# First product of the last token group as seven block products on operand sums, interleaved with the second product of the group ahead

## The chip, the cores and the metric

One NeuronCore of a Trainium2 chip runs the whole program. The metric is the device time of one execution in microseconds, as the median of several runs. A profile is one further execution, with a start and an end for each instruction.

## What is computed

Two stages. The first is an attention with exponential feature maps over 8 batches, 8 heads, 576 positions and 64 columns. The second works on its result, 4608 tokens of 512 numbers:

```python
def _moe_ref(x, g_ln, w_ch1, w_ch2):
    mu = np.mean(x, axis=-1, keepdims=True)
    var = np.mean((x - mu) ** 2, axis=-1, keepdims=True)
    xn = (x - mu) / np.sqrt(var + 1e-06) * g_ln
    ch = np.maximum(xn @ w_ch1, 0.0) @ w_ch2
    return x + ch
```

`w_ch1` is 512 x 2048 and `w_ch2` 2048 x 512. The change concerns the product `xn @ w_ch1` for one ninth of the tokens.

## The kernel before

The tokens form nine groups of 512 (`g` = 0 to 8; `MIX` = 7 holds the last 64 positions of every sequence, `LAST` = 8). Attention for later heads and the two products of earlier groups run interleaved; from about 301 us on only group 7's and group 8's products are left.

**First product** (`first(g, jj)`, L1423 to L1451). The 2048 hidden columns are 16 blocks `jj` of 128. For each block TensorE multiplies four 128x128 pieces of `w1` (one per 128 input numbers) with four 128x512 pieces of the transposed tokens `xT`, summing in one PSUM bank of pool B (`hT_ps`, L1429). ScalarE or VectorE applies the relu on the way to SBUF (L1437, L1439), into `ring`, which holds 24 blocks; the division by the deviation comes later, as the factor `rstd`.

**Second product.** For groups 6, 7 and 8 (`FAST`) it is already done with seven products for eight blocks, after Winograd's form of Strassen's scheme (`fast`, L1537 to L1643). The hidden index is split into even and odd blocks, the output columns into halves of 256, and the token tiles into pairs `p` = 0, 1. `weight_sums` makes four sums of `w2` blocks once, `token_sums` (L1514, instructions on L1531) makes for each pair four sums of `ring` blocks, in two halves of four instructions of 128x512 each. A step `i` = 0 to 6 is eight matmuls of 256 columns (L1594); steps 0 and 1 are split in two halves of four. After each step VectorE multiplies a PSUM range by `rstd` and adds it to the output tile (L1603). For group 7 both PSUM banks of a pair form one tile of pool A, and a later step of the pair waits for VectorE's reading of that tile. Group 7 and 8 each have 28 half or whole pieces, 112 matmuls.

**Order of the work.** The program records operations with the data that they read and write, and a planner (`Order.run`, L365) with assumed durations puts them into one fixed sequence for each engine before the kernel is built. Operations have a rank; `RELU` is the most urgent one. On the chip each engine follows its sequence strictly and waits on semaphores where data or a bank isn't ready. Pool B has three PSUM banks, `n_bank` is one bank, pool A two pairs of banks.

`moe(g)` lists the work. For group 8 it alternates `first(8, jj)` with pieces of `fast(7, ...)`; group 8's token sums come in two halves, after block 8 and after block 15. Then `fast(8, ...)` ends the program, with the output stores on the queues of SyncE and ScalarE. Each output tile of 128 tokens takes one of four slots (`out_pool`), free again when its store is through.

Of the kernel before, what the change touches and what calls it, by code (L numbers as in the profile page):

```python
# [10 lines left out]
FP32 = mybir.dt.float32  # L11
BF16 = mybir.dt.bfloat16
AF = mybir.ActivationFunctionType
ALU = mybir.AluOpType
# [11 lines left out]
RELU = -983.1  # L26
# [300 lines left out]
class Order:  # L327
# [163 lines left out]
def kernel(  # L491
# [27 lines left out]
    HG = 2  # L519
# [17 lines left out]
    EARLY = 8  # L537
    SHARED = 0
    XB = 3
    QB = 4  # L540
    NB16 = 3
    NW = 4
# [15 lines left out]
    ps_B = ctx.enter_context(tc.tile_pool(name="ps_B", bufs=3, space=bass.MemoryType.PSUM))  # L558
# [9 lines left out]
    qx_bufs = [consts.tile([P, TG, 2, D], FP32, name=f"qx{i}") for i in range(2)]  # L568
# [22 lines left out]
    vx_bufs = [consts.tile([P, TG, 2, D1], FP32, name=f"vx{i}") for i in range(2)]  # L591
# [19 lines left out]
    ea_bufs = []  # L611
# [6 lines left out]
    w1_sb = consts.tile([P, KC, DH], BF16, name="w1")  # L618
# [777 lines left out]
    ring = consts.tile([P, HB, RN], BF16, name="hT")  # L1396
# [17 lines left out]
    hT, hkey, ch = {}, {}, {}  # L1414

    def turn_of(g):

        return rk("moe", (H // 2 if g == 0 else H) - 1) if g < NR else counts["V"]

    def due(g, share):  # L1420
        return DUE + BLOCK * (g + share)

    def first(g, jj):  # L1423
        st = {}

        def products():
            st["ps"] = ps_B.tile([P, RN], FP32, tag="B", name="hT_ps")
            for kc in range(KC):
                nc.tensor.matmul(  # L1429
                    st["ps"], w1_sb[:, kc, jj * P : (jj + 1) * P],  # L1430
                    xT_bufs[g % XB][:, kc::KC, :], start=(kc == 0), stop=(kc == KC - 1),
                )

        def relu(engine):
            hT[g, jj] = h_sb = ring[:, slot, :]
            if engine == "DVE":
                nc.vector.tensor_relu(h_sb, st["ps"])  # L1437
            else:
                nc.scalar.activation(h_sb, st["ps"], AF.Relu)  # L1439
# [57 lines left out]
    def weight_sums():  # L1497

        B11, B12 = w2_sb[:, 0::2, 0:FH], w2_sb[:, 0::2, FH:DM]
        B21, B22 = w2_sb[:, 1::2, 0:FH], w2_sb[:, 1::2, FH:DM]  # L1500
        T1, T2, T3, T4 = T_of
        todo = ((T1, B12, B11, ()), (T2, B22, T1, (0,)), (T3, B22, B12, ()), (T4, B21, T2, (1,)))
        for i in range(2):
            add("SP", 0.0, RELU, None, w=[*S_home[i], ("S home", i)])
            add("SP", 0.0, RELU, None, w=[*T_home[i], ("T home", i)])
        for i, (out_, a, b, reads) in enumerate(todo):
            for c in range(0, CP, SH):
                def emit(engine, out_=out_, a=a, b=b, cs=slice(c, c + SH)):
                    eng = nc.vector if engine == "DVE" else nc.gpsimd
                    eng.tensor_tensor(out=out_[:, cs], in0=a[:, cs], in1=b[:, cs], op=ALU.subtract)  # L1510

                add(("DVE", "POOL"), (Port(0.6), 2.0), (), emit,
                    r=[("w2", m) for m in range(NW)] + [("T2", j, c) for j in reads]
                    + [("T home", i // 2)], w=[("T2", i, c)])  # L1514

    def token_sums(g, c):

        for p in range(NM // 2):
            def blocks(i, odd, p=p):
                s = (g * JC + 2 * c) % HB + odd  # L1520
                return ring[:, s : s + 2 * SH - 1 : 2, (2 * p + i) * P : (2 * p + i + 1) * P]

            def sums(i, p=p, blocks=blocks):
                S1, S2, S3, S4 = [t[:, c : c + SH] for t in S_of[p]]
                out_, a, b, op = (
                    (S1, blocks(1, 0), blocks(1, 1), ALU.add),
                    (S2, S1, blocks(0, 0), ALU.subtract),
                    (S3, blocks(0, 0), blocks(1, 0), ALU.subtract),
                    (S4, blocks(0, 1), S2, ALU.subtract),
                )[i]  # L1530
                nc.vector.tensor_tensor(out=out_, in0=a, in1=b, op=op)  # L1531

            for i, reads in ((0, ()), (1, (0,)), (3, (1,)), (2, ())):
                add("DVE", Port(0.32), (), lambda i=i, f=sums: f(i),
                    r=[hkey[g, jj] for jj in range(2 * c, 2 * c + 2 * SH)]
                    + [("S", p, j, c) for j in reads] + [("S home", p)], w=[("S", p, i, c)])

    def fast(g, p, i, cs):
# [104 lines left out]
        elif final:  # L1643
            dma("SP", counts["V"], 262144, lambda: store(g, t, ch["o", g, t]), r=both)

    def moe(g):


        done = 0
        if g == FAST[0]:  # L1650
            weight_sums()
        for jj in range(JC):
            if g <= LAST:
                first(g, jj)
            if g - 1 in FAST:
                pairs_, h1, h2 = range(NM // 2), range(SH), range(SH, CP)
                steps = [(p, i, cs) for cs in (h1, h2) for p in pairs_ for i in range(2)]
                steps += [(p, i, range(CP)) for i in range(2, 7) for p in pairs_]
                until = min(len(steps), -(-(jj + 1) * len(steps) // 8))
                for step in steps[done:until]:  # L1660
                    fast(g - 1, *step)
                done = until
            if g in FAST and jj in (SH * 2, JC - 1):
                token_sums(g, 0 if jj < JC - 1 else SH)
            if g - 1 in FAST:
                continue
            until = min(NM * JC, -(-(jj + 1) * NM * JC // AHEAD_H))
            while g > 0 and done < until:
                i, j0 = divmod(done, JC)
                n = min(until - done, JC - j0)  # L1670
                second(g - 1, i, j0, n)
                done += n
# [183 lines left out]
```

## Time and profile before

| what | value |
|---|---|
| median of 3 runs | 360.21 us (359.09 to 360.39) |
| profiled execution | 359.27 us |
| its span, first to last instruction | 357.5 us |
| around the span | 1.77 us |
| mean granted clock of TensorE | 0.998 |

The profile names engines PE (TensorE), PEld (TensorE's weight loads), DVE (VectorE), ACT (ScalarE), POOL (GpSimd) and SP (SyncE). A group row gives line, engine, instruction, output and inputs, then count, busy time and mean ns of one, and the idle time of the engine just before with what ended it. Durations of instructions that follow one another can overlap: a matmul's row lasts longer than the distance to the next one, and so do VectorE's. What counts for a sum is the distance.

### The profile page before, as it was taken

Reading aid. Unit: us, or ns where it says so; the run is one execution under the profiler, and the core shown is the slowest. Engines: PE = TensorE matmul, PEld = TensorE weight load, DVE = VectorE, ACT = ScalarE, POOL = GpSimd, SP = SyncE. Lnnn points to the kernel's source line nnn. Section 1 sums busy time; section 2 is a strip of 40 time slices with the busy share of each in tenths; the row PEclk is TensorE's granted clock in tenths of the full one; section 3 lists DMA queues with packets and bytes.
Section 4 is the critical chain, followed back from the end, with each engine's and each line's share of the span. In section 5 each row is a group of like instructions: output and inputs, shape, how many; then the busy total and the mean of one; then the engine's idle time right before and its main releaser. Section 6 shows DMA issues by size and latency. Waiting matters only on the chain.

```text
span 357.5 us, 9189 instructions
## 1 busy us (share of the span) xinstructions
PE 348.8 (98%) x3555; PEld 215.5 (60%) x3580; DVE 282.0 (79%) x605; ACT 255.0 (71%) x550; POOL 196.7 (55%) x249
## 2 busy tenths in 40 slices
PE   8999999999999999999999999999999999999995
PEld 8888855555554555455545555555555577457684
DVE  5699989799998888878789999887777897335463
ACT  3998977598988897969696985796788834652320
POOL 5389756596865876648579798465646410000000
PEclk9999999999999999999999999999999999999999
DMA  8999999999996877489629442831041006200503
GB/s 207 308 202 278 205 261 260 242 244 236 296 268 188 199 194 211 114 189 224 193 71 211 64 109 71 171 103 35 9 119 61 3 9 170 67 0 0 119 2 118
DMA packets 93676, 53.89 MB, mean 151 GB/s; under 512 B 61104, under 2 KB 88048, under 8 KB 93632
## 3 DMA queue, kind: packets, MB, share of 16 engines
q1 hardware_dynamic: 89392, 47.72, 55.5%
q0 software_dynamic: 3328, 4.49, 7.2%
q10 hardware_dynamic: 912, 1.08, 1.0%
q8 instruction: 28, 0.46, 0.5%
q14 instruction: 16, 0.13, 0.1%
HBM read 36.77 MB, written 9.44 MB: 129 GB/s over the span
## 4 chain that ended last, share of the span: by engine, by line
PE 79%; DVE 9%; DMA 6%; issue 2%; ACT 2%; SPq 1%; POOL 0%; DVEq 0%
PE hT_ps L1429 30%; PE ch_ps L1461 23%; PE ch L1594 9%; PE pm L988 4%; PE n_bank L1139 3%; PE num L1197 3%; DMA qk<-in_q_dram 2%; PE pt L997 2%; DMA qx<-in_k_dram 2%; DMA out_dram<-o 2%; DVE numc L1219 2%; DVE m L1045 2%; PE n_bank L1133 1%; PE n_bank L1816 1%; ACT ea L1109 1%
## 5 line engine op out<-in xcount | busy, mean ns | idle before, releaser
L1429 PE MATMUL hT_ps<-xT,w 128*128 128x512 bf16 x576 | 137.6, 379 | 0.4 <-DVE hT L1437 0.3
L1461 PE MATMUL ch_ps<-w,hT 128*128 128x512 bf16 x363 | 89.3, 379 | 1.3 <-issue 0.3
L1439 ACT ACTIVATE hT<-hT_ps 128x512 bf16<-128x512 f32 x93 | 55.7, 599 | 43.0 <-PE hT_ps L1429 42.3
L1429 PEld LDWEIGHTS <-w 128*128 128x128 bf16 x576 | 51.8, 98 | 51.8 <-issue 1.6
L1045 DVE TENSOR_REDUCE m<-pm 128x8 f32<-128x1024 f32 x64 | 76.8, 1215 | 7.5 <-PE pm L988 6.4
L1072 POOL TENSOR_TENSOR vv<-v,ek 128x1024 bf16<-128x1024 f32 x32 | 61.0, 1907 | 37.8 <-issue 21.1
L1065 ACT ACTIVATE eb<-pm 128x1024 bf16<-128x1024 f32 x64 | 65.0, 1039 | 5.3 <-DVE m L1045 5.3
L1109 ACT ACTIVATE ea<-pt 128x1024 bf16<-128x1024 f32 x64 | 64.1, 1039 | 3.1 <-PE pt L997 2.7
L1264 POOL TENSOR_TENSOR x<-numc,rden 128x128 bf16<-128x128 f32 (+1 forms) x64 | 39.0, 612 | 40.3 <-DVE rden L1231 34.7
L1461 PEld LDWEIGHTS <-hT 128*128 128x128 bf16 x384 | 34.0, 98 | 34.3 <-issue 0.8
L1437 DVE TENSOR_SCALAR hT<-hT_ps 128x512 bf16<-128x512 f32 x51 | 34.8, 685 | 8.4 <-PE hT_ps L1429 8.0
L1197 PEld LDWEIGHTS <-ea 128*128 128x128 bf16 x512 | 24.5, 97 | 9.9 <-issue 0.7
L900 POOL TENSOR_TENSOR b<-qk,one 128x1024 bf16<-128x1024 f32 x14 | 26.9, 1928 | 4.7 <-issue 1.6
L1139 PE MATMUL n_bank<-vv,eb 128*128 128x65 bf16 x512 | 26.6, 194 | 0.0
L1816 PE MATMUL n_bank<-wz 128*128 128x120 bf16 x355 | 25.1, 224 | 0.2
L1139 PEld LDWEIGHTS <-eb 128*128 128x128 bf16 x512 | 22.3, 98 | 4.5
L1336 DVE BATCH_NORM_STATS2 st<-x 128x6 f32<-128x512 bf16 (+1 forms) x40 | 21.8, 572 | 1.7 <-POOL x L1264 1.5
L1478 POOL TENSOR_TENSOR o<-o,x 128x512 f32<-128x512 f32 x15 | 17.4, 1158 | 10.1 <-ACT o L1474 9.9
L1816 PEld LDWEIGHTS <-wz 128*128 128x128 bf16 x355 | 21.9, 103 | 1.1
L1219 DVE TENSOR_TENSOR numc<-num,em 128x390 f32<-128x390 f32 (+1 forms) x40 | 20.4, 514 | 2.7 <-PE num L1203 1.6
L1225 DVE TENSOR_TENSOR numc<-numc,num 128x390 f32<-128x390 f32 (+1 forms) x40 | 20.5, 516 | 0.5
L1474 ACT ACTIVATE o<-ch_ps,rstd 128x512 f32<-128x512 f32 x15 | 10.3, 687 | 14.3 <-PE ch_ps L1461 14.3
(114 smaller groups left out, 543.3 us busy)
## 6 DMA issues: line engine op xcount, KB each, us to landing
out_dram<-o SPq DMA_DIRECT2D x29, 256.0 KB, 2.4
qk<-in_k_dram SPq DMA_DIRECT2D x12, 512.0 KB, 5.3
qk<-in_q_dram SPq DMA_DIRECT2D x12, 512.0 KB, 6.2
v<-in_v_dram SPq DMA_DIRECT2D x12, 512.0 KB, 4.7
w<-in_moe_w_ch_dram POOLq DMA_DIRECT2D x4, 1024.0 KB, 11.6
qk<-in_k_dram SPq DMA_DIRECT2D x8, 256.0 KB, 8.1
qk<-in_q_dram SPq DMA_DIRECT2D x7, 256.0 KB, 8.1
v<-in_v_dram SPq DMA_DIRECT2D x7, 256.0 KB, 8.1
```

Source lines behind the costliest of these rows:

```text
L1045: nc.vector.reduce_max(out=m, in_=ps, axis=AX.X, apply_absolute_value=True)
L1065: nc.scalar.activation(eb, ps, AF.Exp, scale=(1.0, -1.0)[t])
L1072: eng.tensor_tensor(out=u["vv"][:, :, 0:MX, 0:D], in0=bcast(vb[:, hh, :].rearrange("p (c d) -> p c d", d=D), 1, 2), in1=bcast(e[:, :, 0:MX ...
L1109: nc.scalar.activation(u["EA"][:, t, 0:1024], u["pt"], AF.Exp, scale=(1.0, -1.0)[t])
L1139: nc.tensor.matmul(ps[:, t, c // 4, :], EB[:, t, c, :], vv[:, t, c, :], start=False, stop=(t == 0 and c == MX - 1), skip_group_check=True,)
L1197: nc.tensor.matmul(ps[t][:, i, :], ea(u, t, c), KV[:, t, c // 4, :], start=True, stop=True,)
L1264: eng.tensor_tensor(out=dst, in0=src, in1=by, op=ALU.mult)
L1429: nc.tensor.matmul(st["ps"], w1_sb[:, kc, jj * P : (jj + 1) * P], xT_bufs[g % XB][:, kc::KC, :], start=(kc == 0), stop=(kc == KC - 1),)
L1437: nc.vector.tensor_relu(h_sb, st["ps"])
L1439: nc.scalar.activation(h_sb, st["ps"], AF.Relu)
L1461: nc.tensor.matmul(ch[g, i], hT[g, jj][:, i * P : (i + 1) * P], w2_sb[:, jj, :], start=(jj == 0), stop=(jj == JC - 1),)
L1816: nc.tensor.matmul(warm, wz, wz[:, 0:WN], start=False, stop=False, skip_group_check=True)
```

## The change

The first product of group 8 is done with seven block products for eight. The hidden blocks are split into even and odd (`odd`), the 512 input numbers into halves (`a`) and the tokens into halves of 256 (`b`), and the 16 hidden blocks into four quarters `d` of four blocks.

- `sums_of_w1` (L1706) makes four sums of `w1` blocks on VectorE, for the whole of `w1`: 16 instructions of 128x512 in bf16. They are kept in buffers that attention no longer uses (`b16`, `qkT`, `v`). They are recorded with a late rank and wait for group 8's statistics.
- `sums_of_x` (L1732) makes four sums of group 8's `xT` blocks, 8 instructions of 128x256, kept in `ea` and `eb` buffers.
- `quick(8, d)` does the seven products of a quarter, four matmuls of 256 columns each (L1780): one in `n_bank` (name 1), the others in two banks of pool B (`sum`, names 0 and 2). Bank 0 is added to four times, and after each addition something is read out of it: `keep` (L1812 on VectorE, L1814 on ScalarE) copies a bank to SBUF in fp32, `sum_` (L1797) adds a bank and a kept copy on VectorE into `ring`, `relu` (L1823, L1825) ends a block, once from PSUM and twice in place.
- `quick_moe` alternates these products with `fast(7, ...)` so that `fast` runs `LEAD` = 24 matmuls behind, over all of group 8's first product instead of its first eight blocks. Group 8's token sums are listed behind all of it.
- Group 8's upper eight hidden blocks go into a tile of their own, `late`, instead of `ring`.

`QUICK[MIX]` is empty, so group 7 stays as it was. The core of the diff:

```diff
+    QUICK = {LAST: range(4), MIX: ()}
+    LEAD = 24
...
+    def sums_of_w1(gate):
+        todo = (((1, 0), (1, 1), ALU.add, ()), (0, (0, 0), ALU.subtract, (0,)),
+                ((0, 0), (1, 0), ALU.subtract, ()), ((0, 1), 1, ALU.subtract, (1,)))
...
+                def emit(k, out_=F_of[half][i], a=block(a), b=block(b), op_=op_):
+                    nc.vector.tensor_tensor(out=out_[:, k], in0=a[:, k], in1=b[:, k], op=op_)
+
+                for k in range(2):
+                    add("DVE", Port(0.32), 2000.0 + half, lambda k=k, f=emit: f(k),
...
+    def sums_of_x(g):
+        X1, X2, X3, X4 = X_of[g]
...
+        todo = ((X1, block(0, 1), block(0, 0), ()), (X2, block(1, 1), own(X1), (0,)),
+                (X3, block(1, 1), block(0, 1), ()), (X4, block(1, 0), own(X2), (1,)))
...
+    late = xpool.tile([P, JC // 2, RN], BF16, tag="x", name="late")
...
+                for c in range(2):
+                    for k in range(2):
+                        nc.tensor.matmul(
+                            st[name][:, c, :], left(c, k), right(k), start=start and c + k == 0,
+                            stop=c + k == 2, skip_group_check=True,
+                        )
...
+        products(1, A(0, 1), B(1, 0), True, True, w_keys + x_keys, acquire=("N", 1))
+        yield
+        keep(1)
+        products(0, A(0, 0), B(0, 0), True, True, w_keys + x_keys, acquire=("B", 1))
+        yield
+        sum_(0, 0, 0, 1, even)
+        products(2, S(0), T(0), True, True, F[0] + X[0], acquire=("B", 1))
+        yield
+        keep(2)
+        products(0, S(1), T(1), False, True, F[1] + X[1])
+        yield
+        keep(0)
+        products(0, S(2), T(2), False, True, F[2] + X[2])
+        yield
+        sum_(1, 1, 0, 2, odd)
+        products(0, A(1, 1), T(3), False, True, w_keys + X[3])
+        yield
+        add(("ACT", "DVE"), (0.55, 0.6), RELU, relu(ring_at(1, 0), lambda: st[0]),
+            r=[q_key(0)], w=odd, release=("B", 1))
+        products(2, S(3), B(1, 1), False, True, F[3] + x_keys)
+        yield
+        sum_(0, 1, 2, 0, even, release=("B", 1))
+        wide_ = space[:, s : s + 3 : 2, :]
+        add(("ACT", "DVE"), (0.95, Port(0.4)), RELU, relu(wide_, lambda: wide_), w=even)
+        add(("ACT", "DVE"), (0.55, Port(0.25)), RELU, relu(ring_at(1, 1), lambda: ring_at(1, 1)), w=odd)
...
+    def quick_moe(g):
+        if not QUICK[MIX]:
+            sums_of_w1([("mv", LAST, t) for t in range(NM)])
+        sums_of_x(g)
+        steps, left, right = fast_steps(), 0, -LEAD
+        for d in range(JC // 4):
+            for _ in quick(g, d):
+                right += 4
+                while steps and left < right:
+                    left += len(steps[0][2])
+                    fast(g - 1, *steps.pop(0))
+        for step in steps:
+            fast(g - 1, *step)
+        for c in (0, SH):
+            token_sums(g, c)
```

What this does to the engines' sequences begins at row 482 of VectorE's; before that all five stand as they did.

On TensorE, group 8's first product began with blocks of four 512-column matmuls in turn with four 256-column ones of group 7's second product (`ch`):

```order
L1429 LDWEIGHTS w_132
L1429 MATMUL hT_ps<-xT_140,w_132 128x512
...
L1594 LDWEIGHTS hT
L1594 MATMUL ch_5562<-w_133,hT 128x256
...
L1429 MATMUL hT_ps<-xT_140,w_132 128x512
```

Now three quick products stand first, of the weights with the tokens (`xT`) and of sums with sums (`ea` holds token sums, `b_0` to `b_2` weight sums), then the two kinds alternate; each row stands for four matmuls and their weight loads:

```order
L1780 MATMUL n_bank<-xT_140,w_132 128x256
...
L1780 MATMUL sum<-xT_140,w_132 128x256
...
L1780 MATMUL sum<-ea_127,b_0_145 128x256
...
L1597 MATMUL ch_5598<-w_133,hT 128x256
...
L1780 MATMUL sum<-xT_140,b_2_147 128x256
...
L1780 MATMUL sum<-ea_127,b_1_146 128x256
```

All blocks are of 256 columns now, and group 7's second product is spread over all of group 8's first.

On VectorE, between group 7's last token sums (L1531, into `v_105`) and its first results (L1603) nothing stood:

```order
L1531 TENSOR_TENSOR qk_100<-hT 128x512
L1531 TENSOR_TENSOR v_105<-hT 128x512
L1531 TENSOR_TENSOR qk_100<-hT,qk_100 128x512
L1531 TENSOR_TENSOR v_105<-hT,v_103 128x512
L1603 SCALAR_TENSOR_TENSOR o<-ch_5562,rstd,xm 128x256
L1603 SCALAR_TENSOR_TENSOR o<-ch_5562,rstd,o 128x256
```

Now the reads of group 8's banks (`sum`, `n_bank`) stand among and behind them (`kept`, `qx` and `vx` are kept copies; five rows of token sums are left out):

```order
L1812 COPY kept<-n_bank 128x512
L1534 TENSOR_TENSOR qk_100<-hT 128x512
L1797 TENSOR_TENSOR hT<-sum,kept 128x2x256
L1534 TENSOR_TENSOR qk_100<-qk_100,hT 128x512
...
L1534 TENSOR_TENSOR v_105<-hT,v_103 128x512
L1797 TENSOR_TENSOR hT<-sum,kept 128x2x256
L1797 TENSOR_TENSOR hT<-sum,qx_88 128x2x256
L1797 TENSOR_TENSOR hT<-sum,vx_106 128x2x256
L1812 COPY qx_89<-sum 128x512
L1606 SCALAR_TENSOR_TENSOR o<-ch_5598,rstd,xm 128x256
```

Six reads of PSUM and eight token sums stand ahead of the first result of group 7's second product.

On ScalarE the last rows were relus from PSUM for both groups and the two stores:

```order
L1369 ACTIVATE rstd<-rstd 128x4
L1439 ACTIVATE hT<-hT_ps 128x512 x32
L1383 DMA out_dram<-o 128x512 x2
L1851 UNCONDITIONAL_BRANCH
```

Half of them stay, for group 7, and behind them copies and relus for group 8 alternate; these are the last ones:

```order
L1814 COPY qx_89<-sum 128x512
L1825 ACTIVATE late<-late 128x2x512
L1825 ACTIVATE late<-sum 128x2x256
L1825 ACTIVATE late<-late 128x2x256
L1385 DMA out_dram<-o 128x512 x2
```

The program's last hidden block is ready after two of these in a row, one out of PSUM and one in place.

More of the change, by code (lines that the diff above doesn't have):

```diff
@@ new lines, in sums_of_x, with block, own, emit @@
+    def sums_of_x(g):
+        X1, X2, X3, X4 = X_of[g]
+        xv = xT_bufs[g % XB].rearrange("p (b i a k) t -> p a b k i t", b=2, i=2, a=2)
+        def block(a, b):
+            return xv[:, a, b]
+        def own(x):
+            return x.rearrange("p k (i t) -> p k i t", t=P)
+        add("SP", 0.0, RELU, None, w=[*X_home[g], ("X home", g)])
+        todo = ((X1, block(0, 1), block(0, 0), ()), (X2, block(1, 1), own(X1), (0,)),
+                (X3, block(1, 1), block(0, 1), ()), (X4, block(1, 0), own(X2), (1,)))
+        for i in range(4):
+            out_, a, b, reads = todo[i]
+            def emit(k, out_=own(out_), a=a, b=b):
+                nc.vector.tensor_tensor(out=out_[:, k], in0=a[:, k], in1=b[:, k], op=ALU.subtract)
+            for k in range(2):
+                add("DVE", Port(0.2), RELU if g == LAST else 2001.0, lambda k=k, f=emit: f(k),
+                    r=[("xT", g % XB, kc) for kc in range(KC)] + [("X", g, j, k) for j in reads]
+                    + [("X home", g)], w=[("X", g, i, k)])
@@ new lines, with hT_at, quick, A @@
+    late = xpool.tile([P, JC // 2, RN], BF16, tag="x", name="late")
+    def hT_at(g, jj):
+        return (late, jj - JC // 2) if g == LAST and jj >= JC // 2 else (ring, (g * JC + jj) % HB)
+    def quick(g, d):
+        space, s = hT_at(g, 4 * d)
+        for i in range(4):
+            hT[g, 4 * d + i] = space[:, s + i, :]
+            hkey[g, 4 * d + i] = ("hT late" if space is late else "hT", s + i)
+        even, odd = [[hkey[g, 4 * d + i], hkey[g, 4 * d + i + 2]] for i in range(2)]
+        xv = xT_bufs[g % XB].rearrange("p (b i a k) t -> p a k b i t", b=2, i=2, a=2)
+        half, c0 = divmod(2 * d, 4)
+        st = {}
+        def A(odd_, a):
+            return lambda c, k: w1_part[:, a, k, odd_, 2 * d + c, :]
+        def S(n_):
+            return lambda c, k: F_of[half][n_][:, k, c0 + c, :]
+        def B(a, b):
+            return lambda k: xv[:, a, k, b]
+        def T(n_):
+            return lambda k: X_of[g][n_][:, k, :]
+        x_keys = [("xT", g % XB, kc) for kc in range(KC)]
+        w_keys = [("w1", n_, kc) for n_ in range(NW) for kc in range(KC)]
+        def products(name, left, right, start, stop, r, w=(), acquire=None):
+            def emit():
+                if start:
+                    st[name] = (
+                        n_bank[:, 0 : 2 * FH] if name == 1
+                        else ps_B.tile([P, 2 * FH], FP32, tag="B", name="sum")
+                    ).rearrange("p (c t) -> p c t", c=2)
+                for c in range(2):
+                    for k in range(2):
+                        nc.tensor.matmul(
+                            st[name][:, c, :], left(c, k), right(k), start=start and c + k == 0,
+                            stop=c + k == 2, skip_group_check=True,
+                        )
+            add("PE", mm(4, FH), turn_of(g), emit, r=r, w=[("quick", g, d, name), *w], acquire=acquire,
+                due=due(g, 4 * d / JC) + (0.0 if start and name < 2 else 40.0))
+            counts["V"] += 1.0
+        def ring_at(odd_, t):
+            return space[:, s + odd_ : s + odd_ + 3 : 2, t * 2 * P : (t + 1) * 2 * P]
+        def q_key(n_):
+            return ("quick", g, d, n_)
+        def both(out_, a, b):
+            def emit():
+                nc.vector.tensor_tensor(out=out_, in0=a(), in1=b(), op=ALU.add)
+            return emit
+        def kept(name):
+            if name == 1:
+                st["kept"] = att.tile([P, 2 * FH], FP32, tag="vv", name="kept")
+                t_ = st["kept"]
+            else:
+                t_ = (U_of if name == 0 else W_of)[d % 2]
+            st["kept", name] = t_.rearrange("p (c t) -> p c t", c=2)
+        def keep(name):
+            def emit(engine):
+                kept(name)
+                if engine == "DVE":
+                    nc.vector.tensor_copy(out=st["kept", name], in_=st[name])
+                else:
+                    nc.scalar.copy(out=st["kept", name], in_=st[name])
+            home_ = (U_home, Y_home, W_home)[name][d % 2][0]
+            add(("ACT", "DVE"), (0.55, 0.6), RELU, emit, r=[q_key(name), (home_, "free")],
+                w=[("kept", name, d % 2)], release=("N", 1) if name == 1 else None)
+        def relu(out_, in_):
+            def emit(engine):
+                if engine == "DVE":
+                    nc.vector.tensor_relu(out_, in_())
+                else:
+                    nc.scalar.activation(out_, in_(), AF.Relu)
+            return emit
+        F = [[("F", half, i, k) for k in range(2)] for i in range(4)]
+        X = [[("X", g, i, k) for k in range(2)] for i in range(4)]
+        def sum_(odd_, t, name, other, w, release=None):
+            add("DVE", 0.66, RELU,
+                both(ring_at(odd_, t), lambda: st[name], lambda: st["kept", other]),
+                r=[q_key(name), ("kept", other, d % 2)], w=w, release=release)
+        products(1, A(0, 1), B(1, 0), True, True, w_keys + x_keys, acquire=("N", 1))
[23 more added lines that the diff above has]
+        add(("ACT", "DVE"), (0.55, Port(0.25)), RELU, relu(ring_at(1, 1), lambda: ring_at(1, 1)), w=odd)
```

79 lines of the change are left out of this document (73 added, 6 removed).

## Prediction

> **What bounds the kernel now.** I read the page's busy shares first, then the chain of waits through the end of the run, then busy time by stretch, then the groups by form for prices.
>
> ```profile
> span 357.5 us, 9189 instructions
> PE 348.8 (98%) x3555; PEld 215.5 (60%) x3580; DVE 282.0 (79%) x605; ACT 255.0 (71%) x550; POOL 196.7 (55%) x249
> ```
>
> The chain of waits from 301 us on (start, us, what) is TensorE and almost nothing else:
>
> ```profile
> 301.43 14.68 PE hT_ps L1429 x68
> 316.11 0.44 PE ch L1594 x4
> 316.54 0.86 PE hT_ps L1429 x4
> ...
> 325.21 4.80 PE ch L1594 x44
> 330.01 0.02 issue
> 330.03 4.57 PE ch L1594 x40
> 334.60 6.91 PE hT_ps L1429 x32
> 341.50 12.24 PE ch L1594 x112
> 353.74 0.02 issue
> 353.77 0.48 DVE o L1603
> ```
>
> Group 7's first product runs to 316 us, then group 8's alternates with group 7's second product, then eight blocks of group 8 stand alone (334.60), then its second product. A 512-column matmul costs 14.68 / 68 = 0.2159 us, a 256-column one 12.24 / 112 = 0.1093 us, weight loads included. The only loss is near 330 us: 325.21 to 334.60 is 9.39 us for 84 matmuls that need 84 x 0.1093 = 9.18, so 0.2 us of waiting. Instructions taken from TensorE here come off the end, if nothing else becomes late. How much room the others have:
>
> ```profile
> core 0: us, PE busy (x) PEld busy (x) DVE busy (x) ACT busy (x) POOL busy (x), PEclk, DMA share, GB/s
> 301.00:316.00 15.00, 15.00 (x73) 6.95 (x72) 3.43 (x11) 10.13 (x19) 0.00 (x0) 1.00 0.34 88
> 316.00:341.30 25.30, 25.28 (x173) 16.77 (x172) 11.85 (x30) 8.92 (x15) 0.00 (x0) 1.00 0.19 42
> ```
>
> VectorE is idle for 11.6 of the first 15 us and for half of the next 25; the granted clock is 1.00. The program stands unchanged up to row 482 of VectorE's queue (300.4 us), so everything is decided in the last 57 us.
>
> **TensorE.** Removed: 16 blocks x 4 = 64 matmuls of 512 columns, 64 x 0.2159 = 13.82 us. Added: 4 quarters x 7 products x 4 = 112 of 256 columns, 112 x 0.1093 = 12.24 us. Difference -1.58 us, all of it on the path. The second products keep their counts.
>
> The 112 added matmuls bring 112 weight loads for 64. The price of 0.1093 already holds one load per matmul:
>
> ```profile
> L1594 PEld LDWEIGHTS <-hT 128*128 128x128 bf16 x98 | 9.6, 98 | 3.0
> ```
>
> Load and 256 columns together take 0.109 us, and the load alone 0.098, so loads lie beside the matmul before. The Trainium skill (TensorE: Matmul & The Clock Gate, Part 3, The mechanism) says that a weight load overlaps matmuls in flight only where their row groups differ; all of these use the whole array, so by that rule nothing would be hidden. The row of 112 in 12.24 us disagrees; what a return of that cost would do is the last rival.
>
> **Weight and token sums before the first quick product.** Added to VectorE: 16 sums of 128x512 bf16 (L1706) and 8 of 128x256 (L1732). Rows of like work: the token sums, by form and then in order of time (start, us):
>
> ```profile
> L1531 DVE TENSOR_TENSOR qk<-hT 128x512 bf16<-128x512 bf16 x8 | 3.4, 421 | 18.3 <-ACT hT L1439 18.3
> 342.23 0.42 DVE L1531 TENSOR_TENSOR qk<-hT 128x512 bf16<-128x512 bf16 x1 [7.11 <-ACT hT L1439]
> 342.57 0.42 DVE L1531 TENSOR_TENSOR v<-hT 128x512 bf16<-128x512 bf16 x1
> ```
>
> One lasts 0.42 us but the next starts after 0.34, so 16 take 5.4 us and the eight half-size ones 1.6 to 2.7. They start near 300.4 us and the quick products start at 301.27 + 64 x 0.216 = 315.1. In between VectorE must also do eight token sums of group 7 (2.7) and two results (0.8): 12 us at most, in 14.7. Cost 0, covered by group 7's 64 matmuls. The cover is gone when a weight sum passes about 0.49 us (0.34 + 2.4 / 16), or 0.64 if the idle wait for group 7's first half is used as well.
>
> **The seven-product chain.** Per quarter ScalarE and VectorE had four activations from PSUM; now three copies to SBUF, three sums that read PSUM and a kept copy, a relu from PSUM and two relus in place. On ScalarE 19 instructions, bounded by 0.60 (L1439, quoted below) and by 1.04 for twice the columns, so 15 us at most in 24, replace 16 of 0.60: no bound. VectorE gets 12 sums, 3 copies and 2 relus, about 10 us, on top of 14 results and 16 token sums (11 us): 21 of 24.4 us, in strict order. No row has a 512-column sum of fp32 out of PSUM. The nearest:
>
> ```profile
> L1219 DVE TENSOR_TENSOR numc<-num,em 128x390 f32<-128x390 f32 x32 | 17.6, 554 | 1.1 <-PE num L1197 1.1
> L1219 DVE TENSOR_TENSOR numc<-n_bank,em 128x195 f32<-128x195 f32 x24 | 8.5, 355 | 7.7 <-PE n_bank L1203 7.3
> L1065 ACT ACTIVATE eb<-pm 128x1024 bf16<-128x1024 f32 x64 | 65.0, 1039 | 5.3 <-DVE m L1045 5.3
> L1437 DVE TENSOR_SCALAR hT<-hT_ps 128x512 bf16<-128x512 f32 x51 | 34.8, 685 | 8.4 <-PE hT_ps L1429 8.0
> L1469 DVE SCALAR_TENSOR_TENSOR o<-ch_ps,rstd,x 128x512 f32<-128x512 f32 x9 | 6.7, 745 | 1.2 <-PE ch_ps L1461 0.9
> 246.30 0.55 DVE L1219 TENSOR_TENSOR numc<-num,em 128x390 f32<-128x390 f32 x1
> 246.77 0.35 DVE L1225 TENSOR_TENSOR numc<-numc,n_bank 128x195 f32<-128x195 f32 x1
> ```
>
> From 195 to 390 columns duration grows by 1.02 ns a column, so 512 last 0.554 + 122 x 1.02 = 0.68 us. The one of 390 holds the queue for 0.47 (246.30 to 246.77), 0.08 less than it lasts, so c = 0.60 us per sum. Ends: 0.47 (the 390-column pitch) and 0.745 (L1469, its whole duration). I take 0.60 to 0.66, the sum with the same operation and operand kinds. The Trainium skill (VectorE: DVE Perf Modes, Side-by-side) gives 1x mode as one element a cycle at 0.96 GHz plus about 158 cycles of fill and decode; as an estimate from that page, (512 + 158) / 0.96 = 0.70 us, with which the waits below would come to 0.9 and the whole gain to 0.9 us.
>
> **The tight place.** TensorE's 18th block after the start (second half of group 7's step 1) waits for VectorE's first result of that step. TensorE gets there at 17 x 4 x 0.1093 = 7.43 us. VectorE's queue from the start: the first copy can begin at 0.44 + 0.20 = 0.64 (the 0.20 is from the rows below), and ahead of that result stand six reads of PSUM and eight token sums: 0.64 + 6c + 8 x 0.336. The result lasts 0.48.
>
> ```profile
> 341.13 3.59 PEld L1594 LDWEIGHTS <-hT 128*128 128x128 bf16 x32
> 341.34 3.66 PE L1594 MATMUL ch<-w,hT 128*128 128x256 bf16 x32
> 341.60 0.60 ACT L1439 ACTIVATE hT<-hT_ps 128x512 bf16<-128x512 f32 x1 [0.27 <-PE hT_ps L1429]
> 343.91 0.48 DVE L1603 SCALAR_TENSOR_TENSOR o<-ch,rstd,x 128x256 f32<-128x256 f32 x1
> 344.31 0.42 DVE L1531 TENSOR_TENSOR v<-hT 128x512 bf16<-128x512 bf16 x1
> 329.49 0.48 DVE L1603 SCALAR_TENSOR_TENSOR o<-ch,rstd,xm 128x256 f32<-128x256 f32 x1
> 330.03 1.03 PE L1594 MATMUL ch<-qk,v 128*128 128x256 bf16 x8
> ```
>
> The last block of 512 columns is streamed at 341.34, where the next matmul starts; its reader starts at 341.60, 0.20 to 0.26 later. From VectorE back to TensorE it is 0.06 (329.97 to 330.03; this is the wait found above). So the result ends at 3.81 + 6c and TensorE waits 6c - 3.56: 0.04 us at c = 0.60, 0.40 at 0.66, 0.9 at 0.745. Queued behind that matmul is every further product of both groups. A second place of the same kind is near the end of group 7's second product, where its last step waits for the result of the step before behind four token sums and two sums: about 0.03 at 0.60, 0.2 to 0.3 above 0.68. The bank hand-overs between quarters (three banks for two chains a quarter) I walked through in the same way; they come out just in time at 0.60. I put the new waits at 0.3 us (0 to 1.2). The old wait of 0.2 us goes, since those results stand elsewhere.
>
> **The close.** Group 8's last token sums wait for two activations in a row on ScalarE instead of one: VectorE starts them 1.6 us after the last quick product, where before it was 342.23 - 341.34 = 0.9. TensorE has 32 matmuls, 3.5 us, in between, so 0. Group 7's eight stores move some 5 us later on SyncE:
>
> ```profile
> 332.52 5.03 SPq L1392 DMA_DIRECT2D out_dram<-o  x8
> out_dram<-o SPq DMA_DIRECT2D x29, 256.0 KB, 2.4
> ```
>
> The first go near 337.5 and land 2.4 us later, near 340; group 8 first writes that output slot near 343, and the other three in the same order behind: 0; without that cover VectorE's result, and the matmul that reuses its bank, would be late by what is missing of 3 us. From the last matmul on all is as before.
>
> **Sum.** -1.58 - 0.2 + 0.3 = -1.5 us. The profiled execution took 359.27 us (span 357.5 and 1.77 around it) and would take 357.8. It stands 0.94 below the median of the three runs (360.21); off the median the forecast is **358.7 us**. A measurement here can tell about 0.5%, 1.8 us, from no change, so the likeliest case lies just inside that.
>
> **Rivals.**
>
> *VectorE's queue sets the pace.* 21 of 24.4 us in strict order, each sum standing ahead of a product. At c = 0.745 waits are 1.2 us and 0.6 of the gain is left (359.6); from about c = 0.8 nothing is left, and at 0.9 six reads alone cost 1.8 at the first place and as much again behind it: 3.5 us, slower by 1.7 (361.9). For it: no margin at 7.43 us. Against: the row of the same operation gives 0.60. Chance 0.22, of which 0.06 is slower by over 0.5%.
>
> *The sums of w1 come late: slower.* The kernel's other sums of weights:
>
> ```profile
> L1510 DVE TENSOR_TENSOR qk<-w 128x1024 bf16<-128x1024 bf16 x2 | 3.9, 1943 | 0.0
> L1510 POOL TENSOR_TENSOR qk<-w,qk 128x1024 bf16<-128x1024 bf16 x3 | 7.1, 2381 | 0.1
> ```
>
> At that price 512 columns take 0.97 us. From 0.64 us on, the deciding point, TensorE waits for what is over: 16 x (0.97 - 0.64) = 5.3 us, with the 1.5 saved 360.2 + 3.8 = 364.0. Against it: those two had POOL working on the same sums (second row), and POOL stands at 0.00 from 301 us on, where the token sums take 0.42. Chance 0.04.
>
> *Nothing waits.* The new waits are 0 and the old one gone: -1.8 us, 358.4. This needs c at 0.60 or under everywhere. Chance 0.20.
>
> *The weight loads show.* If a load of 0.098 us were added to each matmul instead of hidden, 48 more of them cost 4.7 us against the 1.6 saved: slower by 3.1, 363.3. The 112 in 12.24 us speak against it. This is what the overlap rule cited above would give. Chance 0.01.
>
> **The numbers.** Forecast 0.53. Range: below, the lowest run shown (359.09) less the full 1.8: 357.3; above, the forecast's upper wait of 1.2 (gain 0.6) off the median gives 359.6 and off the highest run (360.39) 359.8, and a little of the first rival beyond: 360.0. Left out are the slow part of that rival and the two costs on the other side. Since the gain of 1.5 lies 0.3 under the bound of 1.8 and the runs scatter by 1.3, a third of the forecast and half of "nothing waits" come out above the bound: faster 0.28, slower 0.06 + 0.04 + 0.01 = 0.11, the rest, 0.61, within.
>
> **What would show it.** Right: TensorE's matmul pitch in the quick products at 0.109 us; waits inside 315 to 340 us of 0.3 us in all, the largest on a group 7 product about 7.4 us after the start, released by a VectorE result; sums of 128x512 from PSUM lasting 0.68 us; VectorE idle for 2 us or more before the first copy from PSUM; the last matmul 1.5 us earlier. Wrong: sums of 0.75 us or more, weight sums over 0.5, a pitch over 0.12, or a new idle of TensorE between 340 and 346 us.

## The result, and the profile after

| | before | after |
|---|---|---|
| median | 359.77 us (358.75 to 361.06, 9 runs) | 357.63 us (357.03 to 358.38, 9 runs) |
| span of the profiled run | 357.5 us | 355.9 us |
| stretch (see below) | 52.31 us | 50.57 us |

The ratio is 0.9946 [0.9928, 0.9963]: 0.54% faster, between 0.37 and 0.72%. The bound of 0.5%, which the prediction put between "no change" and "faster", lies inside that interval. Three single executions in the experiments below ran at a granted clock of 0.994 or 0.995 and took 362 to 365 us; the times and ratios given there leave them out.

The first lines of the page of the changed kernel:

```profile
span 355.9 us, 9338 instructions
...
PE 347.7 (98%) x3603; PEld 221.1 (62%) x3628; DVE 298.7 (84%) x646; ACT 257.9 (72%) x553; POOL 196.5 (55%) x249
```

TensorE has 48 matmuls more and 1.1 us less of busy time; VectorE has 16.7 us more work in a span that is 1.6 us shorter. Its chain of waits through the end of the run (start, us, what):

```profile
301.54 13.81 PE hT_ps L1431 x64
315.35 0.44 PE n_bank L1780 x4
...
322.78 0.46 PE ch L1597 x4
...
336.77 2.66 PE ch L1597 x24
...
339.87 12.24 PE ch L1597 x112
352.11 0.03 issue
```

The chain is TensorE alone, as before. I call *stretch* the time from the first matmul of group 7's first product to the end of the last matmul: 352.11 - 301.54 = 50.57 us, and before 353.74 - 301.43 = 52.31, so 1.74 us less. The stretch leaves out what comes before it, whose length differs from profile to profile (in the runs of this document the stretch starts between 300.4 and 301.5 us), and so measures an edit here more finely than the time does. In it only two pieces stand out: four matmuls that take 0.46 us at 322.78 instead of 0.44, and 24 that take 2.66 at 336.77 instead of 24 x 0.1093 = 2.62.

The first two of the stretches shown of before, busy time by engine (the same columns):

```profile
301.00:316.00 15.00, 15.00 (x77) 7.33 (x76) 10.32 (x34) 10.25 (x19) 0.00 (x0) 1.00 0.35 90
316.00:341.30 25.30, 25.30 (x234) 22.60 (x232) 21.99 (x49) 12.23 (x19) 0.00 (x0) 1.00 0.12 26
```

VectorE went from 3.43 to 10.32 us in the first and from 11.85 to 21.99 in the second; TensorE is never idle in either. VectorE's queue in order of time (start, us, instruction, and in brackets the idle time before it):

```profile
300.45 0.40 DVE L1706 TENSOR_TENSOR b<-w 128x512 bf16<-128x512 bf16 x1
...
306.00 0.76 DVE L1706 TENSOR_TENSOR v<-w 128x512 bf16<-128x512 bf16 x2
309.11 0.43 DVE L1534 TENSOR_TENSOR qk<-hT 128x512 bf16<-128x512 bf16 x1 [2.36 <-ACT hT L1441]
...
315.83 0.69 DVE L1812 COPY kept<-n_bank 128x512 f32<-128x512 f32 x1 [2.33 <-PE n_bank L1780]
...
319.71 0.69 DVE L1797 TENSOR_TENSOR hT<-sum,kept 128x512 bf16<-128x512 f32 x1
320.31 0.69 DVE L1797 TENSOR_TENSOR hT<-sum,qx 128x512 bf16<-128x512 f32 x1
...
322.11 0.48 DVE L1606 SCALAR_TENSOR_TENSOR o<-ch,rstd,xm 128x256 f32<-128x256 f32 x1
...
340.54 0.43 DVE L1534 TENSOR_TENSOR qk<-late 128x512 bf16<-128x512 bf16 x1 [0.58 <-ACT late L1825]
```

And TensorE around the first quick product and the tight place, and the first matmuls of group 8's second product (the last row):

```profile
315.19 0.60 PE L1780 MATMUL n_bank<-xT,w 128*128 128x256 bf16 x4
...
322.18 0.60 PE L1780 MATMUL sum<-eb,w 128*128 128x256 bf16 x4
322.64 0.60 PE L1597 MATMUL ch<-w,hT 128*128 128x256 bf16 x4
...
339.71 1.91 PE L1597 MATMUL ch<-w,hT 128*128 128x256 bf16 x16
```

What to see: each sum lasts 0.69 us, but they start 0.60 apart (319.71, 320.31). The result that TensorE's 18th block waits for ends at 322.11 + 0.48 = 322.59, and the block starts at 322.64, 0.46 after the one before it, where blocks otherwise follow at 0.437. The chain of six reads and eight token sums is almost in time, 0.03 us late.

### The profile page after: what moved, and what is told of

It reads as the page before. It is cut to its first block, busy times and chain, and to the rows that moved or that the text cites. A ratio compares the mean times of both kernels' runs of the same rounds, so it can differ in the third digit from the quotient of the medians.

```text
span 355.9 us, 9338 instructions
## 1 busy us (share of the span) xinstructions
PE 347.7 (98%) x3603; PEld 221.1 (62%) x3628; DVE 298.7 (84%) x646; ACT 257.9 (72%) x553; POOL 196.5 (55%) x249
## 4 chain that ended last, share of the span: by engine, by line
PE 87%; DVE 7%; ACT 4%; issue 1%; POOL 0%; DVEq 0%
PE hT_ps L1431 30%; PE ch_ps L1463 23%; PE ch L1597 9%; PE pm L990 4%; PE n_bank L1141 4%; PE n_bank L2064 3%; PE num L1199 3%; PE sum L1780 3%; ACT ea L1111 2%; PE pt L999 2%; PE n_bank L1135 1%; DVE numc L1221 1%; DVE m L1047 1%; DVE numc L1227 1%; PE n_bank L1199 1%
## 5 line engine op out<-in xcount | busy, mean ns | idle before, releaser
L1431 PE MATMUL hT_ps<-xT,w 128*128 128x512 bf16 x512 | 122.5, 379 | 0.1
L1431 PEld LDWEIGHTS <-w 128*128 128x128 bf16 x512 | 45.5, 98 | 45.6 <-issue 1.3
L1441 ACT ACTIVATE hT<-hT_ps 128x512 bf16<-128x512 f32 x77 | 46.1, 599 | 25.9 <-PE hT_ps L1431 25.2
L2064 PE MATMUL n_bank<-wz 128*128 128x120 bf16 x355 | 25.9, 228 | 0.1
```

What stands on the lines that cost most here:

```text
L1431: nc.tensor.matmul(st["ps"], w1_sb[:, kc, jj * P : (jj + 1) * P], xT_bufs[g % XB][:, kc::KC, :], start=(kc == 0), stop=(kc == KC - 1),)
L2064: nc.tensor.matmul(warm, wz, wz[:, 0:WN], start=False, stop=False, skip_group_check=True)
```

## The experiments

**The theory.** The gain is TensorE's smaller amount of work, about 0.39 us for each quarter done with seven products (16 x 0.2158 - 28 x 0.1093), and beside it only the old wait of 0.2 us, which goes away. What it needs is that VectorE's reads of PSUM stay hidden, which is so because group 7's second product stands between the quick products; there is no margin left at the 18th block. **Rival A:** the gain, or part of it, comes from spreading group 7's second product over the whole of group 8's first, which also takes the old wait away, and the seven products add little. **Rival B:** VectorE's queue is not the limit that it looks like; the 0.03 us says nothing of how close it is, and the interleaving isn't needed. **Rival C:** the sums of `w1` are hidden however long they get, or not hidden at all.

All results in one table. "Time" is the ratio to the kernel before, with its 95% interval; the stretch comes from one profile each.

| run | quarters as seven products | time | stretch, us |
|---|---|---|---|
| before | 0 | 1 | 52.31 |
| e1_spread_only | 0 | 0.9993 [0.9978, 1.0008] | 52.19 |
| e5_two_quarters | 2 | 0.9968 [0.9953, 0.9984] | 51.37 |
| after | 4 | 0.9946 [0.9928, 0.9963] | 50.57 |
| e6_group7_quarter | 5 | 0.9928 [0.9907, 0.9949] | 50.11 |
| e7_group7_two | 6 | 0.9936 [0.9913, 0.996] | 50.54 |
| e3b_sums_halved | 4 | 0.9966 [0.9952, 0.9979] | 50.94 |
| e4_weight_sums_twice | 4 | 1.0039 [1.0007, 1.007] | 52.95 |
| e2_no_interleave | 4 | 1.0037 [1.002, 1.0054] | 53.66 |
| e3_sums_twice | 4 | 1.016 [1.0129, 1.0192] | 57.63 |

### Only the spreading

Group 8's first product by ordinary blocks again, no sums of operands, and group 7's second product spread over more of them than in the kernel before:

```diff
-        if not QUICK[MIX]:
-            sums_of_w1([("mv", LAST, t) for t in range(NM)])
-        sums_of_x(g)
...
-            for _ in quick(g, d):
-                right += 4
+            for jj in range(4 * d, 4 * d + 4):
+                first(g, jj)
+                right += 7
```

> Group 8's first product is the old one again (sixteen blocks of four 512-column matmuls, relu from PSUM, no operand sums), but group 7's second product is spread over all of it, as in the changed kernel. Theory (the gain is TensorE's smaller count, 64 x 0.2159 against 112 x 0.1093 us): 13.82 + 24.48 us of matmuls from group 8's first one to the program's last, 38.4 to 38.6 us as before, the 0.2 us of old waits at most gained; about 0 to 0.2 us under the kernel before. Rival (the gain is the new spread of group 7's second product): 1.5 us or more under the kernel before, 37 us in that stretch.

Measured: 359.16 us (358.61 to 360.44) beside 359.29 for the kernel before, the ratio's interval holds 1, and the stretch is 52.19. The first and the last long piece of its chain (between them one block of group 8 stands in turn with one or two sets of four matmuls of group 7; its second product is 18 pieces, eight of four matmuls and ten of eight, and not the 28 named above):

```profile
301.25 17.27 PE hT_ps L1431 x80
...
335.87 17.57 PE ch L1597 x160
```

The stretch is 335.87 + 17.57 - 301.25; the 160 matmuls of 256 columns at its end take 17.57 us, 0.08 us more than 160 x 0.1093. The spread isn't quite that of the changed kernel: four blocks of group 8 stand first, 64 of group 7's 112 matmuls stand between the other twelve, and 48 behind the last one. It takes 0.12 us of waiting away and nothing more. It couldn't bring much more in any order: without a wait these matmuls need 128 x 0.2158 + 224 x 0.1093 = 52.10 us, 0.21 less than before. So rival A falls, for 1.62 of the 1.74 us.

### Two quarters instead of four

```diff
+    def plain(g, d):
+        for jj in range(4 * d, 4 * d + 4):
+            first(g, jj)
...
-            for _ in quick(g, d):
+            for _ in quick(g, d) if d < 2 else plain(g, d):
```

> Only the first two quarters of group 8's hidden blocks are done with seven products, the other two as before; all operand sums are still made. Theory (count): 32 x 0.2159 + 56 x 0.1093 + 224 x 0.1093 = 37.5 us from group 8's first matmul to the last, against 38.3 and 36.7 with none and four quarters, with waits of 0.1 to 0.3 us; 0.8 to 1.0 us under the kernel before. Rival (spread): all of the gain already here. Rival (VectorE's queue limits): no clear order by quarters.

Measured: 358.13 us (357.66 to 359.53), stretch 51.37, 0.82 us under spreading alone. Two quarters bring 2 x 0.39 = 0.78 by the theory. The gain goes with the number of quarters, 0, 0.82 and 1.62 us for none, two and four.

### No interleaving

All quick products of group 8 come first and group 7's second product behind them; the planner holds the latter back until the last quick product is placed:

```diff
-    LEAD = 24
+    LEAD = 1000
...
+                    held = op.number in self.held and self.opens
-                    if op.acquire is None or room[op.acquire[0]] >= op.acquire[1]:
+                    if not held and (op.acquire is None or room[op.acquire[0]] >= op.acquire[1]):
```

> The changed kernel with the same products, but TensorE does all of group 8's quick products first and only then group 7's second product. Theory (the interleaving hides the chain: each bank goes to VectorE or ScalarE and back four times a quarter, 0.20 + 0.60 + 0.06 us each, and only two chains run at a time): waits of 2 to 3 us in the quick products, some 0.5 more behind them, time 2.5 to 3.5 us over the changed kernel, so about the kernel before or just over it. Rival (the count alone decides, the interleaving is of no account): the time of the changed kernel.

Measured: 360.34 us (359.91 to 361.27) beside 359.3 before; stretch 53.66, 3.09 more than with the interleaving and 1.35 more than before. Part of its chain (line numbers are some lines higher here; `L1803` is the sum that is L1797 above):

```profile
319.18 0.60 DVE hT L1803
...
322.62 2.43 PE sum L1785 x20
...
325.12 0.59 ACT qx L1820
...
325.74 0.69 DVE late L1803
...
326.45 0.69 DVE late L1803
```

The path to the end runs through a copy on ScalarE and two sums on VectorE, one after the other, with TensorE waiting for them; of the products that are left in the chain, 20 took 2.43 us instead of 20 x 0.1093 = 2.19. In TensorE's timeline the 112 matmuls of the quick products take 14.74 us instead of 12.24, so 2.5 us of the waits lie among them; the rest, about 0.6, lies behind. The seven products are then worse than the blocks that they replace. Rival B falls in its second half: without group 7's work in between, the chain through VectorE and ScalarE is longer than the work saved.

### The sums longer, in two doses

Each PSUM sum as two of 256 columns, which costs VectorE about 0.06 us more per sum, and, in another kernel, each sum issued twice:

```diff
-                nc.vector.tensor_tensor(out=out_, in0=a(), in1=b(), op=ALU.add)
+                for c in range(2):
+                    nc.vector.tensor_tensor(
+                        out=out_[:, c], in0=a()[:, c], in1=b()[:, c], op=ALU.add
+                    )
```

```diff
-                nc.vector.tensor_tensor(out=out_, in0=a(), in1=b(), op=ALU.add)
+                for _ in range(2):
+                    nc.vector.tensor_tensor(out=out_, in0=a(), in1=b(), op=ALU.add)
```

> Each of the twelve sums out of PSUM is split into two of 256 columns, which by the rows of 195 and 390 columns hold the queue for 0.33 us each, 0.66 for 0.60 together. Theory (6c - 3.56, four of the six are sums): the wait at that matmul grows from 0.03 to about 0.27 us, with a second one of 0.1 to 0.2 us later; 0.3 to 0.5 us over the changed kernel. Rival (room in the queue): no wait, same time.

Measured: 358.03 us (356.66 to 358.41), stretch 50.94, 0.37 over the changed kernel. The halves start 0.33 us apart, so two hold the queue for 0.66, as expected. From its chain, the tight place and the second one near the end of group 7:

```profile
319.26 1.68 DVE hT L1798 x6
...
321.84 0.40 DVE o L1606
322.25 0.04 issue
322.29 0.60 PE ch L1597 x4
...
338.17 1.03 PE ch L1597 x8
```

Here the chain itself runs through VectorE's queue up to 322.25, and TensorE waits 0.28 us for the result of L1606. The second place costs 1.03 - 8 x 0.1093 = 0.16. The formula, with four longer sums ahead of the first place, gives 4 x 0.06 + 0.03 = 0.27 there.

> Each of the twelve sums out of PSUM on VectorE is issued twice (the second writes the same again and waits for the first, 0.69 us more). Theory (no room in VectorE's queue): up to the matmul that waits for group 7's first result there are four of them, so the waits to that point sum to 0.03 + 4 x 0.69 = 2.8 us; over all twelve 8.3 us go in, of which some 2 us of VectorE's idle time are used up: 6 to 7 us over the changed kernel. Rival (VectorE's work lies beside TensorE's and has room): under 1 us.

Measured: 364.86 us (363.52 to 365.56), stretch 57.63, 7.06 over the changed kernel. A sum and its repeat hold VectorE's queue for 0.72 us more than a sum alone (the last section has the rows), a little over the 0.69 expected. What TensorE waits for, from 300 us on (in total, times, longest):

```profile
PE ch L1597 <- DVE o L1606: 2.4, 3, 1.8
PE sum L1780 <- DVE hT L1798: 1.9, 3, 0.9
PE sum L1780 <- DVE late L1798: 1.4, 2, 0.7
```

Up to the matmul that waits for group 7's first result the gaps in TensorE's timeline come to 2.91 us, where four doubled sums make 4 x 0.72 = 2.88; over the whole stretch 7.06 was added, where 12 sums make 12 x 0.72 = 8.6 at most. With 0, 0.06 and 0.72 us more per sum, the waits up to the same place were 0.03, 0.28 and 2.9 us: a margin of zero, and rival B falls in its first half too.

### The sums of `w1` twice

```diff
-                    nc.vector.tensor_tensor(out=out_[:, k], in0=a[:, k], in1=b[:, k], op=op_)
+                    for _ in range(2):
+                        nc.vector.tensor_tensor(out=out_[:, k], in0=a[:, k], in1=b[:, k], op=op_)
```

> Each of the sixteen sums of w1 blocks is issued twice, 5.4 us more (6.7 if each repeat waits for the one before to end). VectorE is idle for 4.7 us between them and the first copy out of PSUM. Theory (covered by group 7's first product up to that): 0.7 to 2.0 us of waits at the start of the quick products, and as much over the changed kernel. Rivals: all hidden (0), or none (5.4 to 6.7).

Measured: 360.01 us (359.25 to 361.0, 9 runs), stretch 52.95, 2.38 over the changed kernel. The longest wait of TensorE, and VectorE's queue from the weight sums to the first copy out of PSUM:

```profile
PE n_bank L1781 <- DVE kept L1813: 1.9, 1, 1.9
```

```profile
299.67 0.85 DVE L1707 TENSOR_TENSOR b<-w 128x512 bf16<-128x512 bf16 x2
...
311.56 1.67 DVE L1707 TENSOR_TENSOR v<-w 128x512 bf16<-128x512 bf16 x4
313.15 0.42 DVE L1534 TENSOR_TENSOR qk<-hT 128x512 bf16<-128x512 bf16 x1
...
317.45 0.68 DVE L1813 COPY kept<-n_bank 128x512 f32<-128x512 f32 x1
```

The weight sums now end where group 7's sums begin, 313.15 - 299.67 = 13.48 us after their start. In the changed kernel, where the next instruction could have started at 306.00 + 0.76 - 0.09 = 306.67, it was 306.67 - 300.45 = 6.22, so 7.26 us were added. The idle times there, 2.36 and 2.33 us, with the 0.08 that each instruction overlaps with the next, make a cover of 4.85; 2.41 is left over, and the stretch grew by 2.38 (1.9 of it in the wait shown, most of the rest at the tight place). So the sums do have cover, and of that size: rival C falls on both sides. I had expected somewhat less, because I took 0.34 to 0.42 us for a repeat; as a pair of sum and repeat takes 1.67 / 2 less the overlap, near 0.79, a repeat costs about 0.45.

### Quarters of group 7 as well

One quarter of group 7's first product (blocks 8 to 11), and, in another kernel, two (8 to 15), where no ordinary block of group 7 is left to stand between its quick products:

```diff
-    QUICK = {LAST: range(4), MIX: ()}
+    QUICK = {LAST: range(4), MIX: (2,)}
```

```diff
-    QUICK = {LAST: range(4), MIX: ()}
+    QUICK = {LAST: range(4), MIX: (2, 3)}
...
-            quicks = quick(g, QUICK[g][0])
+            quicks = (x for d in QUICK[g] for x in quick(g, d))
```

> The changed kernel with one quarter of group 7's first product also done with seven products (the sums of w1 are then made before group 7's products, and four more sums of its tokens). Theory (count): 16 x 0.2159 - 28 x 0.1093 = 0.39 us less than the changed kernel, so about 357.2 us or 2.1 to 2.4 under the kernel before, if the weight sums are there in time. Rival (VectorE's queue already sets the pace): its 12 further PSUM reads and copies show as waits of TensorE between 301 and 316 us and the time is that of the changed kernel or above.

Measured: 357.09 us (356.41 to 357.9, 6 runs), stretch 50.11, 0.46 under the changed kernel; the theory has 0.39 and the 0.07 of waits that go. Two pieces of its chain, the start of the stretch and its end:

```profile
300.77 6.91 PE hT_ps L1431 x32
...
337.77 13.11 PE ch L1597 x120
```

The stretch is 337.77 + 13.11 - 300.77 us. After 32 matmuls of group 7's ordinary blocks the quick products start, at 307.7 us instead of 315.4, and the remaining blocks are part of what stands between them. It is the fastest of all the kernels by its trace. By time alone it can't be told from the changed kernel: the intervals overlap.

> As the one before, but with two quarters of group 7 done with seven products, their chains running against each other with less other work between. Theory (count): 0.79 us less of matmuls than the changed kernel; but each chain hands its bank four times to VectorE or ScalarE and back (0.20 + 0.60 + 0.06 us each), and with less between them waits of 0.5 to 1.2 us should appear, so between 0.3 under and 0.4 over the changed kernel. Rival (no bound but the count): 0.8 under it.

Measured: 357.26 us (356.77 to 358.52, 5 runs), stretch 50.54, the same as with four quarters. Two quarters more save 0.78, and waits take 0.75 of it back (the large ones are 0.19 and 0.16 us near 318 us and 0.39 at 325.69):

```profile
323.37 0.61 ACT hT L1825
323.98 0.67 DVE hT L1797
...
325.04 0.61 DVE hT L1797
...
325.69 1.06 PE sum L1780 x8
```

A relu on ScalarE and then two sums on VectorE, with a result of group 7's second product between them, stand in a row ahead of TensorE's next product. With too little other work between the quick products, the chain shows; whether another order of the same two quarters would hide it was not tried.

## Why the prediction was right, and which term was off

The forecast of 358.7 us lay 1.1 above the median of 357.63, which is inside the range of 357.3 to 360.0. Of the 1.1, 0.44 is the kernel before, whose median was 359.77 in these runs and 360.21 in those that the forecast started from; 0.24 is the term of the waits, below. The other 0.4 stands in no row: the stretch shortened by 1.74 and the spans differ by 1.6, the medians by 2.14. Its cause stays open; the ratio's interval (0.37 to 0.72%, 1.3 to 2.6 us) holds all of these.

- **TensorE, -1.58 us: right.** 112 matmuls of 256 columns at 0.437 for four, with no wait, and the numbers of quarters in e1, e5 and the changed kernel give 0.41 us a quarter where 0.395 was worked out.
- **Weight loads hidden: right.** Blocks of four quick products follow at 0.437 us, the pitch of the second product's 256-column matmuls before. Rival "the weight loads show" did not happen. The overlap rule of the Trainium skill (TensorE: Matmul & The Clock Gate, Part 3, The mechanism), read as in the prediction, is not what these rows show; the same section also lets a load into the background weight buffer run ahead, and no run here shows whether that is what happens.
- **The sums of `w1` and `xT` at nothing: right,** and e4 shows why: 4.85 us of idle time in the queue. That is 0.30 for each of 16 weight sums, so the cover is gone at 0.34 + 0.30 = 0.64 us each, the second of the two bounds that were given. (The first, 0.49, took 2.4 us of room where 14.7 less 12 is 2.7.) The eight sums of `xT` took the low end of their price, 1.6 us.
- **The price of a PSUM sum, 0.60 to 0.66 us: right, at its lower end.** The rows start 0.60 apart. The estimate from the Trainium skill (VectorE: DVE Perf Modes, Side-by-side), 0.70 us, agrees with how long such a row lasts, 0.69; it is the distance that counts in a queue.
- **The tight place: right.** The result was to end at 3.81 + 6 x 0.60 = 7.41 us after the start; it ended at 322.59 - 315.19 = 7.40, with no idle time in VectorE's queue from the first copy on.
- **The new waits, 0.3 us: the term that was off.** About 0.07 was measured, 0.03 of it at the tight place and 0.04 at the second one, so the largest wait was not where it was forecast. The formula gave 0.04 at the price from the row of the same operation; I went up to 0.3 to cover prices up to 0.66 and hand-overs that I had walked through by hand. With that the rival "nothing waits", -1.8, describes what happened (-1.74) better than my likeliest case, -1.5. The gain then falls on the bound of 1.8 us instead of 0.3 below it, where "faster" (0.28) and "no change" (0.61) would have deserved about the same chance.
- **The old wait of 0.2: right.** It was 9.39 - 9.18 = 0.21 us, and it is gone: -1.58 - 0.21 + 0.07 = -1.72, beside -1.74 measured. e1 gains only 0.12 because about 0.08 of waiting is left in its last piece.
- **The close: wrong in a detail without a price.** VectorE started group 8's last token sums 0.83 us after the last quick product (340.54, beside the next matmul's start at 339.71), not 1.6: the first of them reads the block that comes straight out of PSUM, and only the second, at 341.06, waits for the relu in place. TensorE had no idle time there. Group 7's stores came at 336.45 instead of 337.5, and group 8's first result at 342.09 waited only for TensorE: nothing, as forecast.
- **VectorE's queue sets the pace: not so, but near.** 0.06 us more per sum already cost 0.37 us in all.

## What to carry to other kernels

Seven products for eight on an engine that is the bound bring what the counts say, as long as the additions stay hidden on other engines; here one eighth fewer columns gave 11.4% less time (12.24 us for 13.82), since two half-width matmuls cost a little more than one full one. Hidden means by order and not by share: a queue with 3 us of idle time in 25 had no margin at one instruction, and only independent matmuls between the products kept its chain off the path. Work out that place with start distances, not durations. Here the price from rows of the same operation was right and the margin on top of it was the error, so such a margin belongs in the range and not in the forecast; this is one case.

## What the runs showed of the hardware

Groups of the changed kernel, from 300 us on (line, engine, instruction, output and inputs, count, busy us, mean ns, idle before):

```profile
L1797 DVE TENSOR_TENSOR hT<-sum,kept 128x512 bf16<-128x512 f32 x2 | 1.4, 688 | 0.0
L1812 DVE COPY kept<-n_bank 128x512 f32<-128x512 f32 x2 | 1.4, 688 | 2.3 <-PE n_bank L1780 2.3
L1814 ACT COPY vx<-sum 128x512 f32<-128x512 f32 x4 | 2.3, 585 | 1.2 <-PE sum L1780 1.2
L1823 DVE TENSOR_SCALAR hT<-hT 128x1024 bf16<-128x1024 bf16 x1 | 0.4, 420 | 0.0
L1825 ACT ACTIVATE hT<-hT 128x1024 bf16<-128x1024 bf16 x1 | 1.1, 1057 | 0.3 <-DVE hT L1797 0.3
```

A sum of PSUM and a kept fp32 copy lasts as long on VectorE as a copy out of PSUM, 0.688 us: the second operand costs nothing that these rows show. ScalarE makes that copy in 0.585. A relu in place of 1024 bf16 columns takes 0.42 us on VectorE and 1.06 on ScalarE.

Where a VectorE instruction does the same work again on the same range as the one before it (e3, e4), the two no longer overlap. From VectorE's queue in e3, where each row is a sum and its repeat:

```profile
319.27 1.41 DVE L1798 TENSOR_TENSOR hT<-sum,kept 128x512 bf16<-128x512 f32 x2
320.59 1.40 DVE L1798 TENSOR_TENSOR hT<-sum,qx 128x512 bf16<-128x512 f32 x2
```

Two sums of 0.69 us one after the other make 1.38, and the pair lasts 1.41: the repeat starts about 0.03 us after its predecessor has ended, where an ordinary sum starts 0.08 before that. The pairs start 1.32 apart, so a sum and its repeat take 0.72 us more than the 0.60 of a sum alone. In e4 a sum of `w1` and its repeat take 0.79 us where two ordinary ones take 0.67. Whether the engine itself holds the repeat or a wait that the program carries was not tested.
